# A two-part kernel (local attention and a state-space convolution): another element order in the tables that its K generator multiplies

## The chip, the cores and the metric

The kernel runs on one core of a Trainium2 chip. The metric is device time in microseconds: the median of three runs, and beside it one profiled execution with its trace. Engines are named as in the profile: PE is TensorE (matmuls), PEld its weight loads, DVE is VectorE, ACT is ScalarE, POOL is GpSimd and SP is SyncE, which issues most DMAs.

## What is computed

The reference has two independent halves, joined along the last axis. Half A is attention with 32 heads of 20 channels over a dilated window of 8 earlier positions (step 2). Half B is a convolution of the input with a kernel `K` that is itself a sum over 192 complex exponentials:

```python
logdA = dt * A                                  # 640 channels x 192 modes, complex
P = exp(logdA[:, :, None] * l[None, None, :])   # l = 0..2047
K = einsum("dn,dnl,dn->dl", Cc, P, dB).real     # 640 channels x 2048 positions
y = irfft(rfft(pad(u)) * rfft(pad(K)))[:L] + u * Dskip
```

The change touches only the computation of `K`.

## The kernel before

**Splitting of K.** A position l is written as a high and a low part (32 values times 64 values), so that exp(logdA·l) is a product of two tables. `Y` holds the 64 low positions and `X` the 32 high ones, each as a real and an imaginary part, for every mode and channel; the coefficients are folded into `X`. For one channel, `K` is then the matrix product of `X` and `Y` over the modes: 32 by 64 values.

**Chunks and steps.** The 640 channels are processed in five chunks of 128 (`c`), each as two halves of 64 (`th`). A half is 16 channels `t` in each of 4 groups `g`. The 192 modes of the four groups lie in 6 blocks of 128 partitions: blocks 0 to 3 hold modes 0 to 127 of one group each, blocks 4 and 5 hold the last 64 modes of two groups each. So per half the tables are `Y` [128, 2, 6, 64, 16] (real and imaginary, block, position, channel) and `X` [128, 2, 6, 16, 32] (channel outside, position inside).

**Table steps (`table_steps`, lines 185 to 267), 18 per half.** PE multiplies pieces of the parameters (`PM`, `PF`) with constant matrices (`RM`, `RF`, line 164 on) into PSUM (`ps_t`, two buffers), through `block` (lines 202 and 205). ACT turns that into tables:

- `gens` (line 215): exponentials `E`, two factors per block and channel.
- `mag(b)` (lines 222 to 226), three times, two blocks each: ACT writes magnitudes `M`, DVE multiplies them by `E` to get the other positions.
- `magx` (lines 235 and 236), two times (four blocks and two): magnitudes `MX` for X, the second half of the positions again by a DVE multiply with `E`.
- `sin(b, which, cs)` (line 248), twelve times: sines and cosines into `Y` or `X`. After the second of a pair DVE multiplies with the magnitudes: lines 254 to 256 for Y, line 260 for X.

**K steps (`kgen_steps`, lines 270 to 294), 8 per half.** For each channel t, part r and group g one matmul with 32 weight columns from `X` and 64 moving columns from `Y`, in one of four column groups of the array: line 286 for blocks 0 to 3, line 289 for blocks 4 and 5 with 64 rows. One half has 128 matmuls of each line. ACT copies the result to `Ksb` (line 292).

**What runs beside it.** `fwd_steps` (lines 376 and 387) and `inv_steps` (line 426) are the transforms of `u` and `K` as matmuls; `Evac` (line 337) copies PSUM to SBUF alternately on DVE and ACT; `prod` (line 417) multiplies spectra on DVE. Line 634 transposes the attention's input, line 654 is its projections, line 583 the last inverse step.

**Order.** `interleave` (line 342) mixes two lists of steps evenly in the program: the table steps of one half with the K steps of the half before and with transform steps (line 535). The framework's scheduler then fixes the order on each engine; `InOrder` (line 28) pins the order of ACT's table work, because ACT loads one function table for exponentials and another for sines. After some 362 us only attention and the last inverse step are left.

The address steps that matter here: at line 286 `rhs=Y[:, r, g, :, t]` walks the 64 positions with a step of 16 elements (32 bytes), and `lhsT=X[:, r, g, t]` takes 32 consecutive elements.

Of the kernel before, what the change touches and what calls it, by code (L numbers as in the profile page):

```python
# [10 lines left out]
A = mybir.AluOpType  # L11
ACT = mybir.ActivationFunctionType
AX = mybir.AxisListType
bf16 = mybir.dt.bfloat16
f32 = mybir.dt.float32
f16 = mybir.dt.float16
i16 = mybir.dt.int16
# [6 lines left out]
SINSC = 2.0 * 3.1415925 / 65536.0  # L24
ASC = 256.0
# [138 lines left out]
def table_consts_np():  # L164
    d = np.eye(16)
    j = np.arange(32)
    RF = np.zeros((128, 4, 512)); RM = np.zeros((128, 800))
    jt = lambda v: (v[None, :, None] * d[:, None, :]).reshape(16, -1)
    tj = lambda v: (v[None, None, :] * d[:, :, None]).reshape(16, -1)
    for cs in range(2):  # L170
        for r in range(2):
            RF[16 * r:16 * r + 16, cs] = jt(j + 0.5)
            sg = 1.0 if cs == 0 else -1.0
            RF[64 + 16 * r:80 + 16 * r, 2 + cs] = tj(sg * 64.0 * j)
            RF[96 + 16 * r:112 + 16 * r, 2 + cs] = tj(sg * np.ones(32))
        RF[32, cs] = RF[32, 2 + cs] = 3076.0 if cs == 0 else 3072.0
    l0 = np.concatenate([32 + np.arange(16), 15 - np.arange(16)])
    a = np.concatenate([jt(l0 / ASC), tj(64 * np.arange(16) / ASC), jt(np.array([16, 1024]) / ASC)], axis=1)
    for r in range(2):
        RM[16 * r:16 * r + 16] = a  # L180
        RM[32 + 16 * r:48 + 16 * r, 512:768] = tj(np.ones(16))
    return RF, RM


def table_steps(tc, pools, R, P, th, order, Y, X, rows=(128, 128), vorder=None):

    nc = tc.nc
    V = nc.vector  # L190
    MM = nc.tensor.matmul
    RF, RM = R
    PF, PM = P
    pool, psp = pools["arena"], pools["psum"]
    M = pool.tile([128, 6, 4, 256], bf16, name="M", tag="M", bufs=1)
    MX = pool.tile([128, 6, 16, 32], bf16, name="MX", tag="MX", bufs=1)
    E = pool.tile([128, 6, 2, 16], bf16, name="E", tag="E", bufs=1)
    steps = []

    def block(ps, blk, Pt, rhs, K=128):  # L200
        if blk < 4:
            MM(ps, lhsT=Pt[0:K, 2 * blk + th, 0:128], rhs=rhs[0:K], start=True, stop=True, skip_group_check=True)  # L202
        else:
            for h in range(2):
                MM(ps[64 * h:64 * h + 64], lhsT=Pt[0:K, 2 * (2 * h + blk - 4) + th, 128:192], rhs=rhs[0:K], start=True, stop=True,  # L205
                   tile_position=(0, 64 * h), skip_group_check=True)

    def new():
        return psp.tile([128, 2, 512], f32, name="ps_t", tag="tb", bufs=2)

    def gens():
        ps = new()
        for blk in range(6):
            block(ps[:, 0, 32 * blk:32 * blk + 32], blk, PM, RM[:, 768:800], rows[0])
        order(nc.scalar.activation(out=E[:].rearrange("p b k t -> p (b k t)"), in_=ps[:, 0, 0:192], func=ACT.Exp))

    def mag(b):
        def run():
            ps = new()
            for i in range(2):  # L220
                block(ps[:, i], 2 * b + i, PM, RM[:, 0:512], rows[0])
            order(nc.scalar.activation(out=M[:, 2 * b:2 * b + 2, 0:4:3], in_=ps[:].rearrange("p i (k x) -> p i k x", k=2), func=ACT.Exp))  # L222
            m4 = lambda k: M[:, 2 * b:2 * b + 2, k].rearrange("p b (j t) -> p b j t", t=16)
            e = E[:, 2 * b:2 * b + 2, 0].unsqueeze(2).to_broadcast([128, 2, 16, 16])
            V.tensor_tensor(out=m4(1), in0=m4(0), in1=e, op=A.mult)
            V.tensor_tensor(out=m4(2), in0=m4(3), in1=e, op=A.mult)
        return run

    def magx(b0, n):
        def run():  # L230
            ps = new()
            for i in range(n):
                block(ps[:, i // 2, 256 * (i % 2):256 * (i % 2) + 256], b0 + i, PM, RM[:, 512:768])
            lo = MX[:, b0:b0 + n, :, 0:16]
            order(nc.scalar.activation(out=lo, in_=ps[:].rearrange("p i (k t j) -> p (i k) t j", k=2, t=16)[:, 0:n], func=ACT.Exp))
            mxi = V.tensor_tensor(out=MX[:, b0:b0 + n, :, 16:32], in0=lo, in1=E[:, b0:b0 + n, 1].unsqueeze(3).to_broadcast([128, n, 16, 16]), op=A.mult)
            if vorder is not None:
                vorder(mxi)
        return run

    def sin(b, which, cs):
        def run():
            ps = new()
            for i in range(2):
                block(ps[:, i], 2 * b + i, PF, RF[:, 2 * which + cs], rows[1] if which == 0 else 128)
            bs = slice(2 * b, 2 * b + 2)
            dst = Y[:, cs, bs, 32:64].rearrange("p a j t -> p a (j t)") if which == 0 else X[:, cs, bs].rearrange("p a t j -> p a (t j)")
            order(nc.scalar.activation(out=dst, in_=ps[:].bitcast(i16)[:, :, 0::2], func=ACT.Sin, scale=SINSC))  # L248
            if cs == 1:
                if which == 0:  # L250
                    lo = Y[:, :, bs, 32:64].rearrange("p r a j t -> p r a (j t)")
                    hi = Y[:, :, bs, 0:32].rearrange("p r a j t -> p r a (j t)")
                    m = lambda k: M[:, bs, k:k + 2].rearrange("p a k x -> p a (k x)").unsqueeze(1).to_broadcast([128, 2, 2, 512])
                    V.tensor_tensor(out=hi, in0=lo, in1=m(0), op=A.mult)  # L254
                    V.tensor_scalar(out=lo[:, 1], in0=lo[:, 1], scalar1=-1.0, scalar2=None, op0=A.mult)
                    V.tensor_tensor(out=lo, in0=lo, in1=m(2), op=A.mult)  # L256
                else:
                    xf = X[:, :, bs].rearrange("p r a t j -> p r a (t j)")
                    mx = MX[:, bs].rearrange("p a t j -> p a (t j)").unsqueeze(1).to_broadcast([128, 2, 2, 512])
                    V.tensor_tensor(out=xf, in0=xf, in1=mx, op=A.mult)  # L260
        return run
    steps.append(gens)
    steps += [mag(b) for b in range(3)]
    steps += [magx(0, 4), magx(4, 2)]
    for b in range(3):
        steps += [sin(b, w, cs) for w in range(2) for cs in range(2)]
    return steps


def kgen_steps(tc, pools, th, Y, X, Ksb):  # L270
    nc = tc.nc
    MM = nc.tensor.matmul
    st = {}

    def part(jp, half, k0):
        def run():
            if half == 0 and k0 == 0:
                st[jp] = pools["psum"].tile([128, 8, 64], f32, name="ps_k", tag="k", bufs=2)
            ps = st[jp]
            for k in range(k0, k0 + 4):  # L280
                t = 8 * jp + k
                for r in range(2):
                    for g in range(4):
                        o = ps[32 * g:32 * g + 32, k, :]
                        if half == 0:
                            MM(o, lhsT=X[:, r, g, t], rhs=Y[:, r, g, :, t], start=(k == 0 and r == 0), stop=False, tile_position=(0, 32 * g), skip_group_check=True)  # L286
                        else:
                            hb = 64 * (g // 2)
                            MM(o, lhsT=X[hb:hb + 64, r, 4 + g % 2, t], rhs=Y[hb:hb + 64, r, 4 + g % 2, :, t], start=False, stop=(r == 1),  # L289
                               tile_position=(hb, 32 * g), skip_group_check=True)  # L290
            if half == 1 and k0 == 4:
                nc.scalar.copy(out=Ksb[:, 16 * th + 8 * jp:16 * th + 8 * jp + 8], in_=ps[:])
        return run
    return [part(jp, half, k0) for jp in range(2) for half in range(2) for k0 in (0, 4)]
# [139 lines left out]
def partB(tc, pools, prm, B_u, B_Dskip, out_b, att):  # L434
    nc = tc.nc
    MM = nc.tensor.matmul
    cn = fft_consts_np()
    usrc = B_u[0].rearrange("(l1 l0) (g ch) -> g l1 l0 ch", l0=64, g=4)
    with ExitStack() as outer:
# [5 lines left out]
        ar = pools["arena"]  # L445
        pools.update(psum=psk)
        order, vorder, sorder = InOrder(tc), InOrder(tc), InOrder(tc)
# [15 lines left out]
        RF, RM = R[:, 0:2048].rearrange("p (k x) -> p k x", k=4), R[:, 2048:2848]  # L463
# [19 lines left out]
        zedr()  # L483
        lnr()
        exp0()
        Y0 = lambda: ar.tile([128, 2, 6, 64, 16], bf16, name="Y0", tag="Y0")
        Y1 = lambda: ar.tile([128, 2, 6, 64, 16], bf16, name="Y1", tag="Y1")
        X0 = lambda: ar.tile([128, 2, 6, 16, 32], bf16, name="X0", tag="X0")
        X1 = lambda: ar.tile([128, 2, 6, 16, 32], bf16, name="X1", tag="X1")
        Yb, Xb = [Y0()], [X0()]  # L490
        fills = table_steps(tc, pools, (RF, RM), P, 0, order, Yb[0], Xb[0], rows=(32, 64), vorder=vorder)
        for st in fills[:6]:
# [394 lines left out]
```

## Time and profile before

| | us |
|---|---|
| median of three runs (573.23, 575.68, 578.89) | 575.68 |
| the profiled execution | 571.97 |
| its span | 570.2 |
| mean granted TensorE clock | 0.924 |

Busy time in the span: PE 430.1 us (75%) with 6929 matmuls, weight loads 266.7 (47%), DVE 410.3 (72%), ACT 342.3 (60%), POOL 35.2 (6%).

How to read it: no engine is full over the whole span, so a mean says little, and stages have to be looked at one by one. Rows of the groups name the line, engine and operation, output and inputs, size and count; behind the first bar come the total busy time and the mean duration of one, behind the second the idle time of the engine before them and what ended it. A PE row's duration is the latency of one matmul; matmuls overlap, so their pace is read from how many start in a stretch. The chain of waits of this trace reaches back to 260.5 us.

### The profile page before, as it was taken

The page shows a single profiled execution, that of the slowest core. Times are in us where ns is not written, and L with a number is a line of the kernel's source. Part 1 is how long each engine was busy: PE and PEld are TensorE (multiplying, and loading weights), DVE is VectorE, ACT ScalarE, POOL GpSimd, SP SyncE. Part 2 cuts the span into 40 slices and gives each one's busy share as a digit, 9 for nine tenths or more (in the row PEclk, how much of TensorE's full clock was granted, in tenths as well). Part 3 has the DMA queues.
Part 4 walks back from the last instruction along what each step waited for, and adds up shares of the span by engine and source line. Part 5 has one row for each costly group of instructions (what it writes and reads, how often), then busy time and mean ns, then how long its engine had stood idle before and what let it go on. Part 6 is the DMA issues. An engine that isn't in the chain of part 4 may idle for free.

```text
span 570.2 us, 15418 instructions
## 1 busy us (share of the span) xinstructions
PE 430.1 (75%) x6929; PEld 266.7 (47%) x6929; DVE 410.3 (72%) x501; ACT 342.3 (60%) x449; POOL 35.2 (6%) x49
## 2 busy tenths in 40 slices
PE   0135794798889798888988887899785679835796
PEld 0013463364556465546554555656552347701354
DVE  3574799869886998699976977232962669699880
ACT  2483683979597969595977595375221534421354
POOL 8700000000000000100000000000000000000000
PEclk9999997899899999899997999799798899955799
DMA  4594324350035203612052059205472150000112
GB/s 118 128 162 168 119 76 151 91 137 12 11 82 159 85 6 81 171 56 82 2 175 49 3 183 264 77 6 190 154 177 92 29 108 15 5 2 1 36 56 98
DMA packets 51674, 51.56 MB, mean 90 GB/s; under 512 B 37384, under 2 KB 48328, under 8 KB 48664
## 3 DMA queue, kind: packets, MB, share of 16 engines
q1 hardware_dynamic: 49720, 49.69, 31.9%
q0 software_dynamic: 1184, 0.89, 0.7%
q8 instruction: 54, 0.88, 0.6%
q10 hardware_dynamic: 704, 0.00, 0.1%
q14 instruction: 12, 0.10, 0.1%
HBM read 32.30 MB, written 18.19 MB: 89 GB/s over the span
## 4 chain that ended last, share of the span: by engine, by line
PE 29%; DVE 9%; ACT 7%; issue 6%; DMA 2%; SPq 0%; ACTq 0%; POOL 0%; DVEq 0%
PE ps_qk L654 7%; PE ps_v L693 4%; DVE prod L763 3%; PE ps_k L289 3%; PE ps_op L781 2%; DVE prod L706 2%; PE ps_k L286 2%; PE ps_ib L583 2%; ACT Y L248 2%; PE ps_l L709 2%; ACT X L248 1%; PE ps_ia L426 1%; PE ps_t L202 1%; PE ps_xt L634 1%; PE ps_ib L577 1%
## 5 line engine op out<-in xcount | busy, mean ns | idle before, releaser
L706 DVE TENSOR_TENSOR prod<-qT,kT 128x5120 bf16<-128x5120 bf16 x16 | 44.7, 2822 | 25.1 <-ACT kT L337 14.3
L248 ACT ACTIVATE X<-ps_t 128x1024 bf16<-128x1024 int16 x60 | 60.6, 1045 | 3.0 <-PE ps_t L202 2.3
L248 ACT ACTIVATE Y<-ps_t 128x1024 bf16<-128x1024 int16 x60 | 59.2, 1041 | 1.2 <-PE ps_t L202 0.6
L202 PE MATMUL ps_t<-R,PF 128*128 128x512 f16 (+1 forms) x160 | 51.8, 421 | 8.4 <-ACT X L248 3.7
L286 PE MATMUL ps_k<-Y,X 128*32 128x64 bf16 x1280 | 51.8, 294 | 2.1 <-issue 1.8
L289 PE MATMUL ps_k<-Y,X 64*32 64x64 bf16 x1280 | 47.7, 291 | 4.4 <-issue 2.4
L763 DVE TENSOR_TENSOR prod<-v,attn 128x2048 bf16<-128x2048 bf16 (+1 forms) x48 | 46.8, 1039 | 3.2 <-PE ps_o L767 2.7
L202 PE MATMUL ps_t<-R,PM 128*128 128x256 f16 (+4 forms) x120 | 23.4, 299 | 33.0 <-DMA PM<-scr 22.5
L337 DVE CAST A<-ps_f 128x1024 bf16<-128x1024 f32 x28 | 34.2, 1220 | 15.4 <-PE ps_f L376 15.2
L337 ACT CAST Ssp<-ps_f 128x1024 bf16<-128x1024 f32 x26 | 26.5, 1021 | 30.5 <-PE ps_f L387 23.1
L289 PEld LDWEIGHTS <-X 64*32 64x32 bf16 x1280 | 34.5, 109 | 19.3 <-issue 16.8
L286 PEld LDWEIGHTS <-X 128*32 128x32 bf16 x1280 | 34.2, 109 | 18.1 <-issue 11.6
L254 DVE TENSOR_TENSOR Y<-Y,M 128x2048 bf16<-128x2048 bf16 x30 | 36.6, 1219 | 6.1 <-ACT Y L248 6.0
L767 PE MATMUL ps_o<-prod,ident 32*32 32x512 bf16 (+1 forms) x768 | 22.5, 453 | 23.8 <-DVE prod L763 23.7
L376 PE MATMUL ps_f<-BD,u 128*64 128x128 bf16 x320 | 23.1, 296 | 22.9 <-DVE A L337 10.3
L256 DVE TENSOR_TENSOR Y<-Y,M 128x2048 bf16<-128x2048 bf16 x30 | 36.6, 1221 | 0.4
L260 DVE TENSOR_TENSOR X<-X,MX 128x2048 bf16<-128x2048 bf16 x30 | 36.6, 1219 | 0.2
L222 ACT ACTIVATE M<-ps_t 128x1024 bf16<-128x1024 f32 x30 | 30.0, 1026 | 8.8 <-DVE Y L256 4.3
L376 PEld LDWEIGHTS <-u 128*64 128x64 bf16 x320 | 20.8, 204 | 27.3 <-issue 27.1
L205 PE MATMUL ps_t<-R,PF 128*64 128x512 f16 (+1 forms) x160 | 25.4, 384 | 5.5 <-ACT Y L248 3.4
L202 PEld LDWEIGHTS <-PM 128*128 128x128 f16 (+1 forms) x120 | 8.6, 102 | 42.8 <-DMA PM<-scr 22.5
L337 DVE CAST Ssp<-ps_f 128x1024 bf16<-128x1024 f32 x14 | 17.1, 1220 | 12.6 <-PE ps_f L387 12.6
(150 smaller groups left out, 852.6 us busy)
## 6 DMA issues: line engine op xcount, KB each, us to landing
Udram<-Ssp SPq DMA_DIRECT2D x5, 1024.0 KB
U<-Udram SPq DMA_DIRECT2D x5, 1024.0 KB
Uw<-Udram SPq DMA_DIRECT2D x10, 512.0 KB
Zdram<-Z SPq DMA_DIRECT2D x5, 1024.0 KB
zq<-Zdram SPq DMA_DIRECT2D x25, 192.0 KB
u<-in_B_u_dram SPq DMA_DIRECT2D x4, 640.0 KB
xn<-in_A_x_dram SPq DMA_DIRECT2D x4, 640.0 KB
out_dram<-ob SPq DMA_DIRECT2D x16, 160.0 KB
```

What stands on the lines that cost most here:

```text
L202: MM(ps, lhsT=Pt[0:K, 2 * blk + th, 0:128], rhs=rhs[0:K], start=True, stop=True, skip_group_check=True)
L248: order(nc.scalar.activation(out=dst, in_=ps[:].bitcast(i16)[:, :, 0::2], func=ACT.Sin, scale=SINSC))
L254: V.tensor_tensor(out=hi, in0=lo, in1=m(0), op=A.mult)
L256: V.tensor_tensor(out=lo, in0=lo, in1=m(2), op=A.mult)
L260: V.tensor_tensor(out=xf, in0=xf, in1=mx, op=A.mult)
L286: MM(o, lhsT=X[:, r, g, t], rhs=Y[:, r, g, :, t], start=(k == 0 and r == 0), stop=False, tile_position=(0, 32 * g), skip_group_check=True)
L289: MM(o, lhsT=X[hb:hb + 64, r, 4 + g % 2, t], rhs=Y[hb:hb + 64, r, 4 + g % 2, :, t], start=False, stop=(r == 1), tile_position=(hb, 32 * g) ...
L337: ins = self.nc.scalar.copy(out=out, in_=in_) if e == "a" else self.nc.vector.tensor_copy(out=out, in_=in_)
L376: MM(ps[64 * r:64 * r + 64, i], lhsT=src_fn(8 * q + i), rhs=BD[:, r], start=(i % 4 == 0), stop=True, skip_group_check=True, tile_position= ...
L654: self.nc.tensor.matmul(ps, lhsT=self.w[w][:, kt, 128 * ct:128 * ct + 128], rhs=rhs(kt), start=(kt == 0), stop=(kt == 4))
L706: self.nc.vector.tensor_tensor(out=pr[:], in0=q4[:, :, :, hs], in1=k4[:, :, :, hs], op=A.mult)
L763: nc.vector.tensor_tensor(out=p2[:, 0:nd], in0=self.v2[:, 8 * b:8 * b + nd, off:off + 256], in1=self.attn[:, hf, w, :].unsqueeze(1).to_bro ...
```

## The change

All tables get a common order: quads of channels outermost (24 quads: 6 blocks of 4), then positions, then the 4 channels of a quad innermost. The constant matrices are permuted to match (`tjt`), and the E table is ordered by factor, then quad, then channel. At the K step the channel becomes `4 * g + t // 4` and `t % 4`.

```diff
-    M = pool.tile([128, 6, 4, 256], bf16, name="M", tag="M", bufs=1)
-    MX = pool.tile([128, 6, 16, 32], bf16, name="MX", tag="MX", bufs=1)
-    E = pool.tile([128, 6, 2, 16], bf16, name="E", tag="E", bufs=1)
+    M = pool.tile([128, 2 * (6 * 512 + 64)], bf16, name="M", tag="M", bufs=1)
+    MX = pool.tile([128, 24, 32, 4], bf16, name="MX", tag="MX", bufs=1)
+    E = pool.tile([128, 2, 24, 4], bf16, name="E", tag="E", bufs=1)
...
     def mag(b):
...
-            for i in range(2):
-                block(ps[:, i], 2 * b + i, PM, RM[:, 0:512], rows[0])
...
-            m4 = lambda k: M[:, 2 * b:2 * b + 2, k].rearrange("p b (j t) -> p b j t", t=16)
-            e = E[:, 2 * b:2 * b + 2, 0].unsqueeze(2).to_broadcast([128, 2, 16, 16])
-            V.tensor_tensor(out=m4(1), in0=m4(0), in1=e, op=A.mult)
-            V.tensor_tensor(out=m4(2), in0=m4(3), in1=e, op=A.mult)
+            for q in range(2):
+                for i in range(2):
+                    block(ps[:, q, 256 * i:256 * i + 256], 2 * b + i, PM, RM[:, 256 * q:256 * q + 256], rows[0])
...
+            e = E[:, 0, 8 * b:8 * b + 8].unsqueeze(2).to_broadcast([128, 8, 16, 4])
+            for o, i in ((64, 0), (3072, 3136)):
+                m = lambda x: M[:, 1024 * b + x:1024 * b + x + 1024].rearrange("p (k j t) -> p k j t", j=32, t=4)[:, :, 0:16]
+                V.tensor_tensor(out=m(o), in0=m(i), in1=e, op=A.mult)
...
     def magx(b0, n):
...
-            mxi = V.tensor_tensor(out=MX[:, b0:b0 + n, :, 16:32], in0=lo, in1=E[:, b0:b0 + n, 1].unsqueeze(3).to_broadcast([128, n, 16, 16]), op=A.mult)
+            mxi = V.tensor_tensor(out=MX[:, 4 * b0:4 * b0 + 4 * n, 16:32], in0=lo, in1=E[:, 1, 4 * b0:4 * b0 + 4 * n].unsqueeze(2).to_broadcast([128, 4 * n, 16, 4]), op=A.mult)
...
     def sin(b, which, cs):
...
-                    lo = Y[:, :, bs, 32:64].rearrange("p r a j t -> p r a (j t)")
-                    hi = Y[:, :, bs, 0:32].rearrange("p r a j t -> p r a (j t)")
-                    m = lambda k: M[:, bs, k:k + 2].rearrange("p a k x -> p a (k x)").unsqueeze(1).to_broadcast([128, 2, 2, 512])
+                    lo = Y[:, :, ks, 32:64].rearrange("p r k j t -> p r k (j t)")
+                    hi = Y[:, :, ks, 0:32].rearrange("p r k j t -> p r k (j t)")
+                    m = lambda q: M[:, 3072 * q + 1024 * b:3072 * q + 1024 * b + 1024].rearrange("p (k z) -> p k z", z=128).unsqueeze(1).to_broadcast([128, 2, 8, 128])
...
-                            MM(o, lhsT=X[:, r, g, t], rhs=Y[:, r, g, :, t], ...)
+                            MM(o, lhsT=X[:, r, 4 * g + t // 4, :, t % 4], rhs=Y[:, r, 4 * g + t // 4, :, t % 4], ...)
...
-        Y0 = lambda: ar.tile([128, 2, 6, 64, 16], bf16, name="Y0", tag="Y0")
+        Y0 = lambda: ar.tile([128, 2, 24, 64, 4], bf16, name="Y0", tag="Y0")
...
-        X0 = lambda: ar.tile([128, 2, 6, 16, 32], bf16, name="X0", tag="X0")
+        X0 = lambda: ar.tile([128, 2, 24, 32, 4], bf16, name="X0", tag="X0")
```

So at the K step both operands are now read with a step of 4 elements (8 bytes): Y's 64 positions (32 bytes before) and X's 32 positions (consecutive before). A magnitude step issues twice as many matmuls of half the width (256 columns). `Y1` and `X1` change like `Y0` and `X0`, the second K matmul like the first, and `sin`'s output and the multiplication of X follow the new shapes. The numbers of DVE and ACT instructions stay the same.

## The prediction

> **What bounds the kernel now.** I read the costliest groups first, then the timeline of PE for the pace of single matmul runs, then the busy time of all engines between the loads of ScalarE's function table, then the chain of waits. The first fence has the page's span line and its two rows of the K generator, then three rows of the list of groups with shapes kept apart.
>
> ```profile
> span 570.2 us, 15418 instructions
> ...
> L286 PE MATMUL ps_k<-Y,X 128*32 128x64 bf16 x1280 | 51.8, 294 | 2.1 <-issue 1.8
> ...
> L289 PE MATMUL ps_k<-Y,X 64*32 64x64 bf16 x1280 | 47.7, 291 | 4.4 <-issue 2.4 <-DVE Y L256 2.0
> ...
> L225 DVE TENSOR_TENSOR M<-M,E 128x512 bf16<-128x512 bf16 x30 | 12.6, 420 | 10.7 <-ACT M L222 10.6
> ...
> L236 DVE TENSOR_TENSOR MX<-MX,E 128x1024 bf16<-128x1024 bf16 x10 | 12.2, 1220 | 3.0 <-ACT MX L235 3.0
> L236 DVE TENSOR_TENSOR MX<-MX,E 128x512 bf16<-128x512 bf16 x10 | 6.8, 684 | 1.4 <-ACT MX L235 1.4
> ```
>
> 2560 matmuls of only 64 columns. A row's mean is a latency, and four column groups run at once, so the pace has to come from the timeline: start, length, engine, line, count.
>
> ```profile
> 202.87 1.57 PE L286 MATMUL ps_k<-Y,X 128*32 128x64 bf16 x45
> ...
> 224.35 1.11 PE L376 MATMUL ps_f<-BD,u 128*64 128x128 bf16 x16
> ...
> 371.38 0.64 PE L376 MATMUL ps_f<-BD,Ksb 128*64 128x128 bf16 x16
> ...
> 457.14 2.39 PE L583 MATMUL ps_ib<-zq,H 32*32 32x160 bf16 x128
> ```
>
> Taking off the last matmul's latency gives the pace. K: (1.57 - 0.30)/44 = 28.9 ns, or 115 ns for a group of four tiles. Line 583, also four tiles with 32 weight columns each: (2.39 - 0.24)/127 = 16.9 ns, 68 ns per four, although it streams 160 columns against K's 64. Line 583 reads consecutive columns; K reads Y with a step of 32 bytes. Line 376 shows the same on the weights: 64 columns taken from u with a step of 320 bytes go at (1.11 - 0.30)/15 = 54 ns, from Ksb, where they are consecutive, at (0.64 - 0.23)/15 = 27 ns. So widely stepped reads slow PE here: 115 ns for 64 columns is 1.8 ns a column.
>
> Where this matters the windows tell. ScalarE alternates between the exponential table (E, M, MX) and the sine table. Columns: length, then busy us of PE, PE weight load, DVE, ACT, POOL, and the granted clock.
>
> ```profile
> 73.85:99.71 25.86, 18.44 (x362) 13.47 (x359) 24.27 (x64) 14.46 (x22) 1.38 (x1) 0.84 0.31 96
> 114.86:126.25 11.39, 11.39 (x255) 7.89 (x255) 7.26 (x11) 8.07 (x10) 0.52 (x1) 1.00 0.52 146
> 126.25:138.96 12.71, 9.39 (x104) 4.35 (x103) 10.67 (x11) 12.63 (x14) 0.00 (x0) 1.00 0.23 35
> 138.96:155.96 17.00, 14.94 (x306) 10.18 (x306) 15.16 (x23) 10.20 (x12) 1.25 (x1) 0.90 0.02 4
> 172.44:183.75 11.31, 11.31 (x238) 8.07 (x230) 7.61 (x12) 8.49 (x11) 0.00 (x0) 1.00 0.59 149
> 198.93:213.56 14.63, 13.69 (x294) 9.68 (x287) 13.60 (x22) 10.11 (x13) 1.25 (x1) 1.00 0.02 5
> 229.81:243.41 13.60, 11.06 (x212) 7.76 (x200) 9.10 (x8) 7.58 (x10) 0.00 (x0) 0.87 0.55 131
> 258.84:274.60 15.76, 14.73 (x311) 9.95 (x314) 13.95 (x19) 9.49 (x12) 0.00 (x0) 1.00 0.11 35
> 274.60:288.54 13.94, 12.05 (x146) 7.21 (x142) 13.82 (x17) 13.90 (x16) 0.00 (x0) 1.00 0.01 1
> 288.54:300.83 12.29, 10.48 (x234) 7.08 (x230) 6.75 (x11) 7.59 (x10) 0.00 (x0) 0.95 0.78 231
> 316.34:333.41 17.07, 15.01 (x306) 10.19 (x306) 15.19 (x23) 10.20 (x13) 0.00 (x0) 0.90 0.01 2
> 346.20:362.60 16.40, 13.99 (x315) 10.49 (x315) 7.69 (x8) 6.14 (x8) 0.04 (x1) 0.90 0.82 245
> ```
>
> The two sine stretches shown (from 126.25 and 274.60) have ACT busy 99%; the other sine stretches 86 to 98%. Few K matmuls lie there (4 to 72 in each by the counts of lines 286 and 289). The other ten rows are the exponential stretches and the last one, and they hold almost all of K: by the same counts 252, 218, 252, 174, 240, 158, 229, 202, 252 and 252 matmuls. In them ACT has room, and PE or DVE is the full engine. In the last, the chain of waits is half K:
>
> ```profile
> by line: PE ps_k L289 26.7%; PE ps_k L286 24.3%; PE ps_xt L634 18.7%; issue 13.9%; ACT Y L248 10.5%; PE ps_t L205 4.6%; PE ps_f L376 3.9%; PE ps_qk L654 1.8%
> ```
>
> **The change, part by part.**
>
> Y is read with 8 bytes instead of 32. No row has PE reading at 8 bytes, so I bound it. Not better: 115 ns per four, if the slow pace belongs to any step. Best: 64/160 of line 583's 68 ns, 27 ns. Between: if two neighbouring columns together cost what one costs now, 115/2 = 58 ns. Weights bound it too: line 376 with Ksb loads two times 64 columns in 55 ns, so four times 32 columns need about 55 as well if they go one after another. I take 60 ns, 15.0 ns per matmul, near line 583's 16.9, the only four-tile row without a step. That saves 13.9 ns each, 35.6 us of PE over 2560.
>
> [...]
>
> X's weights go from consecutive to a step of 8 bytes. At best free. At worst each column pays like u's: 54 ns for 64 columns is 27 ns for 32, still under today's 28.9 per matmul. So this edit can take the gain away, but cannot by itself make K slower. I take it as covered by the streaming.
>
> MX's multiply (line 236) now has four consecutive E values innermost instead of one repeated. 1024 elements cost 1220 ns now; the product with U at line 417, the same size but consecutive, costs 688, and 512 elements at line 225 cost 420 against 684. If four-element rows count as consecutive, a table set saves 0.53 + 0.26 = 0.80 us of DVE. Lines 225 and 226 have the opposite risk: their E rows shrink from 16 elements to four. Bounds: nothing, or 684 instead of 420, 0.26 us x 60 = 16 us of DVE. I take nothing, since the 16-element rows already run at the fast price.
>
> The Y multiplies go from rows of 512 to rows of 128, same elements. The casts of A (rows of 8) and Ssp (rows of 256) both cost 1220 ns, so row length is free. ScalarE's outputs change pattern, not size: M in pieces of 256 costs 1026 ns, X in one piece 1045; zero.
>
> Magnitude matmuls: 80 of 512 columns become 160 of 256. From zero (same columns) to 80 x 27 ns = 2.2 us; I take 1 us.
>
> The built program has the same instructions otherwise, in an order that shifts in places, on SP only around the writes of Ssp and the pieces. Like stretches differ today by about 1.2 us around their mean (11.3 to 13.6; 14.6 to 17.1); nine of them with random signs make 3.6, so 4 us either way.
>
> Sum. Each stretch can gain at most the K saving, DVE's idle time plus the 0.8 of MX, or ACT's idle time, whichever is least. From 73.85: 2.4 (DVE), 3.0, 2.6 (DVE), 2.4, 1.8 (DVE), 2.2, 2.6 (DVE), 2.8, 2.7 (DVE), 3.5; together 26.0 us. An engine driven to zero idle is not what in-order queues give, so I take in full only the three where PE holds the end (114.86, 172.44 and the last: 8.9), and half of the five under DVE (12.1) and of the two where PE itself idles 15 to 19% (5.0): 8.9 + 6.0 + 2.5 = 17.4. Less 1 for the split: 16.4. The sine stretches gain nothing; after 362.6 us no part of the change is left. The profiled execution took 571.97 us (span 570.2 plus 1.8 around it), 3.7 below the median of 575.68. So 555.6 against it, 559 on the median's scale. What is late next is DVE's multiply of Y (line 256), for which K's second half waits already (2.0 us in its row).
>
> **The rivals.**
>
> Nothing on PE: X's stepped weights, or the 8-byte step itself, keep 115 ns. Then only MX is left, 0.8 us in five stretches under DVE, half of it, 2 us: 574. For it: a weight load one after another at u's rate costs as much as now. Against: u's step is 320 bytes.
>
> More: reading at 27 ns and weights in parallel. K saves 22 ns each; limits then give 3.3 + 2.8 + 5.6 in the PE stretches and 10 in the others: 21.7, so about 555, and 546 if all caps of 26 and the spread of 4 come together.
>
> Slower: the clock. If shorter K bursts leave PE idle and its clock is cut, every consecutive stream is slower. PE's busy time from 74 to 362.6 us is 245.5, of it 82 K, so 164 scale with the clock, whose mean there is 0.94. At 0.70 that is 164 x (0.94/0.70 - 1) = 56 us, half on the path 28, less 16.4: 587. It decides from a mean of 0.78 down (34 us, half 17). For it: 0.52 and 0.62 are seen between 500 and 540 us, where PE starves. Against: the row with PE's lowest share among those shown for sines, 126.25 at 74%, has clock 1.00.
>
> [...]
>
> **How the numbers follow.** Forecast 0.62 (551 to 567), more 0.12, nothing 0.16, slower 0.10. From the 26 us ceiling plus spread, 546, rounded to 547, up to 577 (574 and the spread of the runs shown, about 3): only the slower case and the tails lie outside. About 1%, 5.8 us, is what a measurement can tell: faster 0.74, same 0.16, slower 0.10.
>
> **What would show it.** K runs at 14 to 17 ns per matmul, and exponential stretches 1 to 3 us shorter while sine stretches stay; the 1024-element MX multiply near 690 ns, M's near 420; X's weight loads not much above 109 ns; clock near 0.94 until 362 us. It is wrong if K stays at 28 ns, or if K is fast and the stretches keep their length because DVE's line 256 ends them, or if M's multiplies cost 680.

## The result, and the profile after

The changed kernel takes 556.01 us (median of 4 runs, 555.12 to 558.34), the kernel before, run beside it, 574.45 us (4 runs): a ratio of 0.9715 with an interval of 0.9636 to 0.9794. A second comparison on another chip, with more runs, gave 0.9778 [0.9730, 0.9826], 557.41 against 569.79 us. Ratios compare means and leave out every run more than 1.5% above the fastest of its kernel, so they are not the quotients of the medians. The profiled execution took 555.12 us; the kernel before had 571.97 in its own.

First the page of the changed kernel: its span and the two K rows (busy us, mean ns of one, then the idle time before them).

```profile
span 553.3 us, 15581 instructions
...
L288 PE MATMUL ps_k<-Y,X 128*32 128x64 bf16 x1280 | 31.7, 240 | 4.4 <-issue 2.4
...
L292 PE MATMUL ps_k<-Y,X 64*32 64x64 bf16 x1280 | 27.6, 234 | 4.3 <-issue 2.8
```

K had 51.8 + 47.7 = 99.5 us of PE before and has 59.3 now. The list of groups with shapes kept apart has the multiplies of DVE and X's weight loads:

```profile
L228 DVE TENSOR_TENSOR M<-M,E 128x512 bf16<-128x512 bf16 x60 | 22.3, 418 | 4.2 <-ACT M L224 3.8
...
L238 DVE TENSOR_TENSOR MX<-MX,E 128x1024 bf16<-128x1024 bf16 x10 | 6.9, 688 | 2.9 <-ACT MX L237 2.9
L238 DVE TENSOR_TENSOR MX<-MX,E 128x512 bf16<-128x512 bf16 x10 | 4.2, 416 | 1.0 <-ACT MX L237 1.0
...
L288 PEld LDWEIGHTS <-X 128*32 128x32 bf16 x1280 | 22.8, 118 | 16.8 <-issue 9.3 <-DVE X L262 3.7 <-DVE Y L258 0.8
```

MX's multiplies fell from 1220 and 684 ns to 688 and 416, M's stayed at 418. The timeline of PE has the pace (start, length, engine, line, count, and the idle time before, if any):

```profile
308.99 1.42 PE L288 MATMUL ps_k<-Y,X 128*32 128x64 bf16 x79
...
311.98 1.15 PE L292 MATMUL ps_k<-Y,X 64*32 64x64 bf16 x64 [0.52 <-DVE Y L258]
```

(1.42 - 0.24)/78 = 15.1 ns per matmul for the first half of K, (1.15 - 0.23)/63 = 14.6 for the second, against 28.9 before. The second line also shows what K waits for now: DVE's second multiply of Y.

The busy time of all engines in the nine exponential stretches, and last from the start of the first of them to the last K matmuls, with all that lies between (length, PE, PE weight load, DVE, ACT, POOL, granted clock, DMA share, GB/s):

```profile
74.83:102.09 27.26, 18.05 (x396) 13.79 (x393) 24.85 (x65) 14.98 (x22) 1.41 (x1) 0.81 0.31 91
117.13:125.32 8.19, 6.29 (x218) 4.65 (x218) 5.04 (x10) 6.47 (x8) 0.56 (x1) 1.00 0.96 233
138.35:152.96 14.61, 11.15 (x316) 8.71 (x316) 14.34 (x23) 9.78 (x12) 1.38 (x1) 1.00 0.03 7
168.91:180.89 11.98, 11.65 (x304) 8.86 (x303) 8.19 (x13) 9.21 (x12) 0.16 (x1) 1.00 0.55 146
193.86:208.36 14.50, 11.20 (x316) 8.79 (x316) 14.21 (x23) 9.78 (x12) 1.38 (x1) 1.00 0.03 7
224.30:233.70 9.40, 8.38 (x225) 6.44 (x225) 8.53 (x5) 7.31 (x10) 0.17 (x1) 0.82 0.79 202
249.92:262.18 12.26, 10.02 (x258) 7.22 (x258) 12.26 (x19) 9.32 (x12) 0.00 (x0) 1.00 0.01 3
276.08:284.28 8.20, 7.24 (x221) 5.21 (x219) 6.04 (x11) 7.27 (x9) 0.00 (x0) 1.00 0.83 288
301.73:317.65 15.92, 12.55 (x321) 10.07 (x321) 13.96 (x22) 9.78 (x12) 0.00 (x0) 0.79 0.01 3
...
74.83:347.00 272.17, 211.15 (x4172) 143.76 (x4168) 228.31 (x313) 216.49 (x247) 12.38 (x9) 0.94 0.35 99
```

Set against the rows of before, stretch by stretch, in us:

| stretch | 1 | 2 | 3 | 4 | 5 | 6 | 7 | 8 | 9 | sum |
|---|---|---|---|---|---|---|---|---|---|---|
| before | 25.86 | 11.39 | 17.00 | 11.31 | 14.63 | 13.60 | 15.76 | 12.29 | 17.07 | 138.9 |
| after | 27.26 | 8.19 | 14.61 | 11.98 | 14.50 | 9.40 | 12.26 | 8.20 | 15.92 | 122.3 |
| change | +1.40 | -3.20 | -2.39 | +0.67 | -0.13 | -4.20 | -3.50 | -4.09 | -1.15 | -16.6 |

All of the gain is in the exponential stretches. The sine stretches between and before them together went from 155.2 to 156.1 us. From the last load of the sine table to the end of the last K matmul it took 28.9 us before and 29.6 after, and from there to the end of the span 208 and 206. So K's tail, in which half of the chain of waits was K, is no shorter. Stretch 5 is as long as it was: DVE is busy 14.21 of its 14.50 us, and PE, busy 11.20 us there for 13.69 before, spends idle what the faster K saves it.

### The profile page after: what moved, and what is told of

Read it like the earlier page. It is cut to its first block, busy times and chain, and to the rows that moved or that the text cites. A ratio compares the mean times of both kernels' runs of the same rounds, so it can differ in the third digit from the quotient of the medians.

```text
span 553.3 us, 15581 instructions
## 1 busy us (share of the span) xinstructions
PE 397.3 (72%) x7009; PEld 254.0 (46%) x7009; DVE 401.4 (73%) x501; ACT 339.5 (61%) x449; POOL 35.2 (6%) x49
## 5 line engine op out<-in xcount | busy, mean ns | idle before, releaser
L709 DVE TENSOR_TENSOR prod<-qT,kT 128x5120 bf16<-128x5120 bf16 x16 | 44.7, 2822 | 27.4 <-ACT kT L340 14.5
L250 ACT ACTIVATE Y<-ps_t 128x1024 bf16<-128x1024 int16 x60 | 59.3, 1042 | 1.7 <-PE ps_t L203 0.9
L340 DVE CAST A<-ps_f 128x1024 bf16<-128x1024 f32 x28 | 34.1, 1218 | 22.5 <-PE ps_f L379 22.5
L203 PE MATMUL ps_t<-R,PM 128*128 128x256 f16 (+3 forms) x160 | 23.3, 265 | 35.8 <-DMA PM<-scr 23.5
L256 DVE TENSOR_TENSOR Y<-Y,M 128x2048 bf16<-128x2048 bf16 x30 | 36.5, 1217 | 7.4 <-ACT Y L250 7.4
L258 DVE TENSOR_TENSOR Y<-Y,M 128x2048 bf16<-128x2048 bf16 x30 | 36.6, 1219 | 0.3
L288 PE MATMUL ps_k<-Y,X 128*32 128x64 bf16 x1280 | 31.7, 240 | 4.4 <-issue 2.4
L203 PEld LDWEIGHTS <-PM 128*128 128x128 f16 (+1 forms) x160 | 13.2, 100 | 43.0 <-DMA PM<-scr 23.5
L292 PE MATMUL ps_k<-Y,X 64*32 64x64 bf16 x1280 | 27.6, 234 | 4.3 <-issue 2.8
L288 PEld LDWEIGHTS <-X 128*32 128x32 bf16 x1280 | 22.8, 118 | 16.8 <-issue 9.3
L429 PE MATMUL ps_ia<-IA,U 128*128 128x128 bf16 x160 | 23.4, 227 | 4.7 <-DVE Z L340 3.5
L203 PEld LDWEIGHTS <-PF 128*128 128x128 f16 (+1 forms) x160 | 14.0, 102 | 27.8 <-issue 22.1
```

The source lines that it names most:

```text
L258: V.tensor_tensor(out=lo, in0=lo, in1=m(1), op=A.mult)
L288: MM(o, lhsT=X[:, r, 4 * g + t // 4, :, t % 4], rhs=Y[:, r, 4 * g + t // 4, :, t % 4], start=(k == 0 and r == 0), stop=False, tile_positio ...
L292: MM(o, lhsT=X[hb:hb + 64, r, kq, :, t % 4], rhs=Y[hb:hb + 64, r, kq, :, t % 4], start=False, stop=(r == 1), tile_position=(hb, 32 * g), s ...
L340: ins = self.nc.scalar.copy(out=out, in_=in_) if e == "a" else self.nc.vector.tensor_copy(out=out, in_=in_)
L709: self.nc.vector.tensor_tensor(out=pr[:], in0=q4[:, :, :, hs], in1=k4[:, :, :, hs], op=A.mult)
```

## The experiments

Three questions stand behind the gain of 13 to 16 us (by the two ratios). Is it K's pace, and what in the read sets that pace? Is it MX's multiply? Is it the order of the instructions? The last one can't be left aside: a different operand step also makes the build put the instructions in a different order. Two orders matter below. "The changed order" is that of the changed kernel. "The other order" is the one that came about where X's weights were read consecutively, or at 32 bytes, with Y at 8 or 32; some 1330 of the 7009 matmul places differ between the two (here and below: the matmuls in order of time, told apart by the names of what they write and read).

Most variants change only what K's matmuls read, by one helper that cuts a channel's 64 (or 32) positions out of the same table with a step of n elements; n = 4 is the changed kernel's own read:

```python
def steps_y(Y, ps, r, b, t, n):
    f = lambda a, w: Y[ps, r, a:a + w].rearrange("p k j t -> p (k j t)")
    if n == 16:
        return f(4 * b, 4)[:, t::16]
    if n == 8:
        return f(4 * b + 2 * (t // 8), 2)[:, t % 8::8]
    q = f(4 * b + t // 4, 1)
    if n == 4:
        return q[:, t % 4::4]
    m = q.shape[1] // 4 * n
    o = m * ((t % 4) // n)
    return q[:, o + t % n:o + m:n]
```

Each diff below shows the first half of K; the second half has the same edit.

**Y at 32 bytes, X at 8, in the changed order.**

```diff
-rhs=Y[:, r, 4 * g + t // 4, :, t % 4]
+rhs=steps_y(Y, slice(0, 128), r, g, t, 16)
```

> The changed kernel, but K's moving operand is taken from Y with a step of 32 bytes again (the elements read are others, so K's values are not the reference's; counts, sizes and the order on every engine are those of the changed kernel). Theory, the pace of K is the gain: K returns to 27 to 29 ns per matmul and the time to about 572 us (574.5 before, less 2 for MX), ratio 0.99 to 1.00. Rival, the cheaper MX multiply on DVE or the new order on the engines is the gain: K is slow again but the time stays within 555 to 562 us, ratio below 0.98.

Measured: 569.33 us (10 runs) against 569.24, ratio 1.0009 [0.9972, 1.0046]. The timeline of PE in this kernel shows K back at the old pace, (2.59 - 0.30)/78 = 29.4 ns:

```profile
320.93 2.59 PE L302 MATMUL ps_k<-Y,X 128*32 128x64 bf16 x79
```

All the other parts of the change are in this kernel: MX's cheap multiply (687 ns), the split magnitude matmuls, the new order. Together they are worth nothing that these runs resolve (2 us either way). What the change gains hangs on the step of Y.

**Y at 16 bytes**, a single run:

```diff
-rhs=steps_y(Y, slice(0, 128), r, g, t, 16)
+rhs=steps_y(Y, slice(0, 128), r, g, t, 8)
```

> The changed kernel with Y read with a step of 16 bytes (other elements, so K's values are not the reference's; same counts and order). Theory, neighbouring columns share a fetch of 16 bytes: 16 bytes is as slow as 32, 27 to 29 ns per matmul. Rival, the cost grows with the step: between 15 and 28, about 19 ns. Second rival, weights set the changed kernel's pace and the reading is free up to some step: 14 to 16 ns.

Measured: 567.67 us. Half the step, the same pace, (2.57 - 0.30)/78 = 29.1 ns:

```profile
321.75 2.57 PE L302 MATMUL ps_k<-Y,X 128*32 128x64 bf16 x79
```

**Y and X consecutive:**

```diff
-MM(o, lhsT=X[:, r, 4 * g + t // 4, :, t % 4], rhs=Y[:, r, 4 * g + t // 4, :, t % 4],
+MM(o, lhsT=steps_y(X, slice(0, 128), r, g, t, 1), rhs=steps_y(Y, slice(0, 128), r, g, t, 1),
```

> The changed kernel with both K operands read consecutively (other elements, so K's values are not the reference's; same counts, the scheduler shifts the order a little). Theory, reading Y two columns to a fetch sets the 14 to 15 ns: K falls below 14, to 7 if streaming alone were left. Rival, four weight loads one after another set it (13.8 ns each by the Ksb row): K stays at 13 to 15 ns. On the time: if PE still holds the stretches, another 3 us per ns 1.2 saved, 550 to 553 us at 10 ns; if DVE and ACT have taken over, 555 to 557.

Measured: 547.11 us (4 runs), ratio 0.9611 [0.9570, 0.9652], with K at (0.73 - 0.20)/68 = 7.8 ns, in an order that differs from the other one in some 950 places.

```profile
327.24 0.73 PE L302 MATMUL ps_k<-Y,X 128*32 128x64 bf16 x69
```

This is 6 to 10 us below the changed kernel by the ratios, but two things changed with it, the pace and the order. The next runs part them.

**Y consecutive, X left at 8 bytes**, a single run:

```diff
-rhs=Y[:, r, 4 * g + t // 4, :, t % 4]
+rhs=steps_y(Y, slice(0, 128), r, g, t, 1)
```

> The changed kernel with Y read consecutively and X still with a step of 8 bytes (Y's elements are others, so K's values are not the reference's; same counts, order shifted a little). With both consecutive K went at 7.8 to 9.2 ns. Theory, the four weight loads run side by side and are hidden: again 8 to 10 ns. Rival, X's step costs as much as Y's did: 13 to 15 ns as in the changed kernel.

Measured: 562.26 us against 570.33. K is as fast as with both consecutive, (0.69 - 0.205)/59 = 8.2 ns, and yet the kernel is slower than the changed one. The timeline of PE, and the windows over the table stretches (columns as above):

```profile
316.93 0.69 PE L302 MATMUL ps_k<-Y,X 128*32 128x64 bf16 x60
```

```profile
74.50:355.30 280.80, 211.60 (x4168) 139.84 (x4166) 228.84 (x313) 217.97 (x247) 12.35 (x9) 0.87 0.33 96
```

X's weights with a step of 8 bytes don't hold K at 15 ns. The granted clock is 0.87 here where the changed kernel has 0.94. Some 270 of the matmul places differ from the changed order, so this single run doesn't tell the clock from the order.

**Channel pairs instead of quads, in the changed order to the instruction.** All tables have pairs innermost, so that both operands are read with a step of 4 bytes.

```diff
-    tjt = lambda v: (v[None, None, :, None] * d.reshape(16, 4, 1, 4)).reshape(16, -1)
+    tjt = lambda v: (v[None, None, :, None] * d.reshape(16, 8, 1, 2)).reshape(16, -1)
...
-    MX = pool.tile([128, 24, 32, 4], bf16, name="MX", tag="MX", bufs=1)
-    E = pool.tile([128, 2, 24, 4], bf16, name="E", tag="E", bufs=1)
+    MX = pool.tile([128, 48, 32, 2], bf16, name="MX", tag="MX", bufs=1)
+    E = pool.tile([128, 2, 48, 2], bf16, name="E", tag="E", bufs=1)
...
-MM(o, lhsT=X[:, r, 4 * g + t // 4, :, t % 4], rhs=Y[:, r, 4 * g + t // 4, :, t % 4],
+MM(o, lhsT=X[:, r, 8 * g + t // 2, :, t % 2], rhs=Y[:, r, 8 * g + t // 2, :, t % 2],
```

> The same change with channel pairs in place of quads: 48 pairs outermost, then positions, then 2 channels, so K reads both operands with a step of 4 bytes. Nothing is left out. Theory, cost by fetches of 16 bytes, now four columns each: 8 to 10 ns per matmul, as fast as consecutive, and the multiplies by E, with rows of two, keep 418 and 688 ns: 547 to 551 us, faster than the changed kernel by about 1%. Rival, rows of two elements lose the packed rate on DVE (684 and 1220 ns, 24 us more): 556 us or more. On the time a second rival, PE no longer matters: 555 to 557.

Measured: 560.69 us (6 runs), ratio 0.9818 [0.9774, 0.9863], no better than the quads (0.9778 on another chip), and above both the 547 to 551 us of the theory and the 555 to 557 of the second rival. K runs at (0.83 - 0.20)/78 = 8.1 ns; M's and MX's multiplies keep their price (419, 689 and 420 ns). The timeline, then the windows of one exponential stretch (the fifth) and of all:

```profile
311.39 0.83 PE L288 MATMUL ps_k<-Y,X 128*32 128x64 bf16 x79
```

```profile
194.10:208.70 14.60, 10.38 (x315) 7.51 (x315) 14.08 (x22) 9.99 (x12) 1.04 (x1) 0.88 0.02 4
...
74.40:350.00 275.60, 202.98 (x4171) 134.54 (x4170) 229.20 (x313) 217.41 (x247) 12.35 (x9) 0.90 0.34 98
```

PE is 8 us less busy than after the change (203.0 against 211.2), and the stretches together are 3.4 us longer. The fifth has DVE full in both kernels (14.08 of 14.60, 14.21 of 14.50), so a faster K has little to give there. And the clock is lower: 0.90 over all, 0.88 in the fifth, where it was 1.00. How much of the missing gain is DVE and how much the clock was not told apart.

**Single channels outermost**, both operands consecutive, and every row of E one repeated element (the same edit as for pairs, with one channel):

```diff
-    tjt = lambda v: (v[None, None, :, None] * d.reshape(16, 4, 1, 4)).reshape(16, -1)
+    tjt = lambda v: (v[None, None, :, None] * d.reshape(16, 16, 1, 1)).reshape(16, -1)
```

> The same change with single channels outermost, so K reads both operands consecutively and E's innermost row is one repeated element. Nothing is left out. K goes at 8 to 9 ns as with consecutive reads. Theory, the multiplies by E lose the packed rate: 684 ns for M, 1220 and 684 for MX, 24 us of DVE in the exponential stretches, of which a third to two thirds shows: 555 to 565 us, slower than pairs. Rival, DVE has room: 547 to 551 us, like pairs.

Measured: 562.18 us (6 runs), ratio 0.9823 [0.9772, 0.9874]. The list of groups shows M's multiplies at the price that the prediction had as their upper bound:

```profile
L228 DVE TENSOR_TENSOR M<-M,E 128x512 bf16<-128x512 bf16 x60 | 38.0, 685 | 5.4 <-ACT M L224 5.3
```

They cost 15.7 us more of DVE than after the change, MX's (1218 and 684 ns) 8 more. The time lies in the expected range, but it is not slower than pairs, as had been expected. Against the kernel with the same consecutive reads and cheap multiplies (0.9611), the ratio is 0.021 higher, 12 us. That would make DVE worth about half its price, but the orders of these two were not matched, and below an order alone is worth 5 to 9 us; so what DVE's 24 us cost in time is not shown. Shown is that rows of four or of two E values are what keeps M cheap (418 and 419 ns, for 685 here).

**MX's multiply dear again**, all else as changed:

```diff
-in1=E[:, 1, 4 * b0:4 * b0 + 4 * n].unsqueeze(2).to_broadcast([128, 4 * n, 16, 4])
+in1=E[:, 1, 4 * b0:4 * b0 + 4 * n, 0:1].unsqueeze(2).to_broadcast([128, 4 * n, 16, 4])
```

> The changed kernel with MX's multiply reading one repeated E element innermost, as before the change (the factor of each first channel of a quad for all four, so MX is not the reference's). It should cost 1220 and 684 ns again, 8 us more of DVE. Theory, MX is a small part of the gain: 557 to 560 us. Rival, the stretches are bound by DVE now (it is busy 98% of two of them): 5 us or more, 561 us and up.

Measured: 557.41 us (4 runs), ratio 0.9807 [0.9744, 0.9871], with MX at the old price:

```profile
L238 DVE TENSOR_TENSOR MX<-MX,E 128x1024 bf16<-128x1024 bf16 x10 | 12.2, 1221 | 2.9 <-ACT MX L237 2.9
```

Of the changed kernel's two ratios, 0.9778 lies inside that interval and 0.9715 just below it, with an interval of its own up to 0.9794. MX's multiply is worth less than these runs resolve, and some 280 matmul places moved with it.

**The changed kernel again**, beside the next three on one chip:

> The changed kernel itself once more, to stand beside the next three on one chip and beside pairs. Theory, K's pace is worth 16 to 17 us in this order: ratio to before 0.97. If pairs (0.982) are really slower than quads, it lies below 0.977; if that was chance, near 0.98.

Measured: 557.41 us (6 runs) against 569.79 (17 runs), ratio 0.9778 [0.9730, 0.9826]. That is between the two values expected; whether pairs are really slower than quads stays open.

**X consecutive, Y at 8 bytes, in the other order:**

```diff
-MM(o, lhsT=X[:, r, 4 * g + t // 4, :, t % 4],
+MM(o, lhsT=steps_y(X, slice(0, 128), r, g, t, 1),
```

> The changed kernel with X's weights read consecutively (other elements, so K's values are not the reference's). In the built program every engine has the same work, but in the order of the run with X at 32 bytes, which is nearer to that of the kernel before. Theory, the step of X's weights costs nothing on PE but turned the scheduler to a worse order: K at 14 to 15 ns as in the changed kernel and yet 547 to 551 us. Rival, the one look at 550 us was chance: 555 to 557 us, as the changed kernel.

Measured: 548.97 us (6 runs), ratio 0.9614 [0.9559, 0.9668]. K's pace in its timeline is (1.26 - 0.24)/68 = 15.0 ns:

```profile
325.33 1.26 PE L302 MATMUL ps_k<-Y,X 128*32 128x64 bf16 x69
```

The same pace as the changed kernel, 8.4 us less; and the same ratio as with both consecutive (0.9611), where K ran at 7.8 ns, so below 15 ns nothing more came out here either, though these two orders differ in some 950 places. X's 8-byte step costs PE nothing that can be seen, but its edit changed the order, and the order costs.

**X consecutive, Y at 32 bytes, in the other order to the instruction:**

```diff
-rhs=Y[:, r, 4 * g + t // 4, :, t % 4]
+rhs=steps_y(Y, slice(0, 128), r, g, t, 16)
```

(and X as in the run before)

> As the last, with X consecutive and Y at 32 bytes (other elements, so K's values are not the reference's): the order of the last run to the instruction, K at its old pace of 27 to 29 ns. Theory, pace and order add: 563 to 567 us, 4 to 6 below the kernel with the changed order and the old pace, and 15 to 17 above the last run. Rival, the order is only better with a fast K: 568 to 571, as the kernel before.

Measured: 564.75 us (10 runs), ratio 0.9914 [0.9879, 0.9949], K at (2.29 - 0.29)/68 = 29.4 ns:

```profile
341.63 2.29 PE L302 MATMUL ps_k<-Y,X 128*32 128x64 bf16 x69
```

With this run the two causes stand in a square (ratios to the kernel before, 29 ns on the left, 15 on the right; the upper row has X at 8 bytes, the lower X consecutive):

| | Y at 32 bytes | Y at 8 bytes | pace |
|---|---|---|---|
| changed order | 1.0009 | 0.9778 | 13 us |
| other order | 0.9914 | 0.9614 | 17 us |
| order | 5 us | 9 us | |

The intervals of the four ratios leave 3 to 4 us either way on each difference. So pace and order are both clear of the noise, and whether the order is worth more with a fast K is not.

**X at 32 bytes, Y at 8**, a single run, in the other order:

```diff
-MM(o, lhsT=X[:, r, 4 * g + t // 4, :, t % 4],
+MM(o, lhsT=steps_y(X, slice(0, 128), r, g, t, 16),
```

> The changed kernel with X's weights read with a step of 32 bytes and Y with 8 (X's elements are others, so K's values are not the reference's; same counts and order). Theory, weights and Y are read side by side, and 32 lone fetches of 1.8 ns take 58 ns, as long as Y's 64 columns in pairs: 14 to 17 ns per matmul. Rival, weight loads of the four column groups share one reader: 4 x 58 ns per four, 50 ns or more per matmul; or they add to Y's reading: 25 to 30 ns.

Measured: 550.26 us against 570.33. The list of groups and the timeline of PE:

```profile
L302 PEld LDWEIGHTS <-X 128*32 128x32 bf16 x1280 | 28.7, 163 | 13.4 <-issue 6.8 <-DVE X L262 2.9 <-DVE Y L258 0.8
```

```profile
329.10 1.39 PE L302 MATMUL ps_k<-Y,X 128*32 128x64 bf16 x69
```

A weight load takes 163 ns where the consecutive one (X consecutive, Y at 8 bytes) has 108, and K goes at (1.39 - 0.245)/68 = 16.8 instead of 15.0 ns. The changed kernel, with X at 8 bytes, has 118 and 15.1 ns: four times the step on the weights costs 2 ns, and the same on Y 14. The time goes with the order and not with X's step: with the dearest weight loads of all it is 0.965 of the kernel before, like X consecutive (0.961) and unlike X at 8 bytes in the changed order (0.978). So the order, and not the step of X, parts the two rows of the square, as far as a single run can tell.

**Y, M and E in quads, X and MX in single channels.** It keeps Y's 8-byte step, gives X its consecutive read back, and pays for it with MX's dear multiply.

```diff
+    tjx = lambda v: (v[None, None, :, None] * d.reshape(16, 16, 1, 1)).reshape(16, -1)
...
-    MX = pool.tile([128, 24, 32, 4], bf16, name="MX", tag="MX", bufs=1)
+    MX = pool.tile([128, 96, 32, 1], bf16, name="MX", tag="MX", bufs=1)
...
-MM(o, lhsT=X[:, r, 4 * g + t // 4, :, t % 4],
+MM(o, lhsT=X[:, r, 16 * g + t // 1, :, t % 1],
...
-        X0 = lambda: ar.tile([128, 2, 24, 32, 4], bf16, name="X0", tag="X0")
+        X0 = lambda: ar.tile([128, 2, 96, 32, 1], bf16, name="X0", tag="X0")
```

> Y, M and E as in the changed kernel, but X and MX with single channels outermost and positions innermost, so X's weights are consecutive again and nothing is left out. MX's multiply costs 1220 and 684 ns again, 8 us more of DVE. The order is within 191 of 7009 matmul places that of the two runs before. Theory, order is worth more than MX's multiply: 549 to 554 us, faster than the changed kernel. Rival, MX's multiply takes back what the order gives: 555 to 558 us.

Measured: 549.84 us (6 runs), ratio 0.9658 [0.9608, 0.9708]: 7.6 us below the changed kernel on the same chip, and below both kernels, though MX costs 1222 and 685 ns again. K runs at (1.14 - 0.24)/62 = 14.5 ns, and the stretches show the old clock:

```profile
328.26 1.14 PE L290 MATMUL ps_k<-Y,X 128*32 128x64 bf16 x63
```

```profile
73.00:340.00 267.00, 210.75 (x4180) 139.43 (x4177) 236.34 (x314) 218.80 (x249) 12.51 (x10) 0.94 0.36 102
```

DVE does 8 us more than after the change (236.3 against 228.3), and from the first exponential stretch to the last K matmul it takes 264.8 us instead of 272.4: the better order gives more than MX's multiply takes.

## Why the prediction was right, and where it was not

**K's pace.** The step that carried the forecast was the choice of 60 ns per four tiles, because "two neighbouring columns together cost what one costs now". The trace after has 15.1 and 14.6 ns for 15.0. The runs show the same thing as a law of this case: 29 ns at 32 and at 16 bytes, 15 at 8, and 8 both at 4 bytes and consecutive. That fits a cost by the number of 16-byte pieces that the columns lie in, 29 ns for 64 of them, half for 32, and a floor near 8 ns for 16 and for 8; it is a reading of these steps alone. Where a piece begins and what makes the floor were not tried.

**The other reason for the 60 was wrong.** "Weights bound it too", at about 55 ns per four, does not hold: in pairs K takes 4 x 8.1 = 32 ns per four, and with Y consecutive and X still at 8 bytes 4 x 8.2 = 33. That bound agreed with the right value by chance.

**X's weights, taken as covered.** They are: K's pace is the same with X consecutive (15.0 ns). But X's edit was not free. It came with another order, and between the two orders lie 5 to 9 us, more than any term of the sum but K's.

**MX, M, Y, ScalarE, the split magnitude matmuls.** 688, 416 and 418 ns for the forecast 688, 420 and 420; the Y multiplies 1217 and 1219; ACT's X in 1047. With K slow again all of this together, order included, gave 1.0009, so the 2 us that were left for MX alone and the 1 us against the split are inside the noise or cancelled by the order.

**The order, 4 us either way.** For the order that was built this held: with a slow K, order and all other parts together are worth nothing (1.0009). As a measure of what an order can do it was too small. It was taken from how much like stretches differ, with random signs; between the two orders it is 5 us with a slow K and 9 with a fast one, and the sign is one that the build decides.

**The caps.** The sum, 16.4 us, and 555.6 us against the profiled execution, met 555.12. Its parts did not meet theirs. That an engine keeps some idle time, from which the halves were taken, was an estimate: DVE is busy 12.26 of 12.26 us in stretch 7 after the change. The first two rows set the prediction's terms, stretch by stretch, against the kernel before and the one after. That difference mixes pace with order. The last two hold the order fixed: from Y at 32 bytes to the changed kernel, and in the other order from Y at 32 to Y at 8 with X consecutive. All are us gained, read from the loads of the function tables; the changed kernel's repeat differs by up to 1.0 us in a stretch.

| stretch | 1 | 2 | 3 | 4 | 5 | 6 | 7 | 8 | 9 | sum | sine stretches between | tail |
|---|---|---|---|---|---|---|---|---|---|---|---|---|
| predicted | 1.2 | 3.0 | 1.3 | 2.4 | 0.9 | 1.1 | 1.3 | 1.4 | 1.4 | 14.0 | 0 | 3.5 |
| before to after | -1.4 | 3.2 | 2.4 | -0.7 | 0.1 | 4.2 | 3.5 | 4.1 | 1.1 | 16.6 | 0.2 | -0.6 |
| pace, changed order | 2.7 | 0.2 | 0.9 | 2.5 | 0.8 | 1.4 | 1.0 | 1.4 | -0.2 | 10.7 | 3.2 | 0.4 |
| pace, other order | 1.8 | 2.4 | 1.6 | 0.3 | 0.9 | 0.9 | 1.4 | 1.4 | 2.1 | 12.8 | 2.4 | 0.5 |

With the order held, the pace gave 11 to 13 us in the exponential stretches for the 14 counted, 2 to 3 us in the sine stretches, for which nothing was counted, and half a microsecond in the tail for 3.5. That the total was met is in part luck: the sine stretches made up for most of the tail. The gains of 4.2, 3.5 and 4.1 us in stretches 6, 7 and 8, above their caps of 2.2, 2.6 and 2.8, are mostly the order: with a slow K in the changed order these stretches already take 10.85, 13.29 and 9.55 us, where they had 13.60, 15.76 and 12.29, because work moved between stretches (DVE has 5 instructions in the sixth, where it had 8). The fourth, taken in full because PE was full in it, did gain 2.5 from the pace in the changed order; the new order hid it.

**The tail.** The step that failed is its 3.5 us "in full". The chain of waits named K as half of it, and K at half its time left the length nearly as it was: from the last load of the sine table to the last K matmul 30.0 us with Y at 32 bytes in the changed order (30.2 at 16) and 29.6 after (28.9 in the repeat), 26.4 and 25.9 in the other order; the kernel before, in an order of its own, took 28.9. The order has a share in the length, 3 to 4 us: the other kernels in the changed order or near it take 28.6 to 28.9, all others after the change 25.0 to 26.7. What took K's saving can be read in the two traces of the changed order. From the first K matmul after the wait for X (348.48 and 335.14 us) to the end of the last one both take 12.1 us. With the slow K, PE is busy 11.7 of them, with the fast one 8.1, and at one and the same matmul of the transposes it stands still for 0.4 us in the first and 3.5 us in the second:

```profile
356.95 0.23 PE L651 MATMUL ps_xt<-ident,xn 128*128 128x128 bf16 x1 [0.40 <-issue]
...
344.34 0.25 PE L637 MATMUL ps_xt<-ident,xn 128*128 128x128 bf16 x1 [3.52 <-issue]
```

In the other order it is 0.6 us with the slow K and 3.0 with the fast one, again at one place in the order:

```profile
350.00 0.75 PE L306 MATMUL ps_k<-Y,X 64*32 64x64 bf16 x18 [0.63 <-issue]
...
334.04 0.46 PE L306 MATMUL ps_k<-Y,X 64*32 64x64 bf16 x18 [3.00 <-issue]
```

So K gave PE the time back (some 250 matmuls at 14 ns, 3.6 us), and PE stood still for most of it. The 13.9% "issue" in the prediction's chain of waits is for the most part such a standstill, of 2.1 us ahead of 356.42 us; the sum took no account of it. What it may be stands in the last section.

**What is late next** was named rightly in part. DVE is full in stretches 3, 5 and 7 (14.34 of 14.61, 14.21 of 14.50, 12.26 of 12.26 us), and the pairs show that K below 15 ns has nothing more to give in this order. But the wait that was named, for DVE's second multiply of Y (line 256 before, 258 now), is 1.6 us in the row of K's second half, less than its 2.0 before, and "issue" in that row has 2.8.

**The rivals.** "Nothing on PE" is refuted by the pace, and the run with Y at 32 bytes shows what it would have been: no change, 1.0009, where 574 of 575.68 (0.997) had been worked out. "More" came about in the pairs as far as the reading goes, 32 ns per four, but its further gain of 4 us did not. "Slower by the clock" did not happen, 0.94 before and after, but a lower clock comes with a shorter K: 0.90 in pairs, 0.87 with Y consecutive, 0.91 with both consecutive. A low clock comes without a single long gap too: in the kernel before, PE is busy 1.38 of the 3.41 us from 145.89 on, idle in pieces of at most 1.5 us, and the granted clock of the next 3.41 us is 0.50. PE's busy time alone does not settle it: from 466.75 on it is 1.38 of 3.41 us as well, and the clock stays at 1.00. What the lower clock costs in time was not told apart; with both consecutive the kernel is one of the two fastest all the same.

## What to carry to other kernels

Lay out a matmul's moving operand so that the columns of one read lie close together: here 1, 2 and 4 columns to 16 bytes gave 29, 15 and 8 ns, while on the weights, with X consecutive at 15.0 ns, a step of 8 bytes gave 15.1 and one of 32 bytes 16.8. Take such a layout change apart by operand: keep the step on the one that needs it, and leave the other as it was. Before a layout is judged by its time, look at whether the build put the instructions in another order with it; here that was worth 5 to 9 us, a third to a half of what the layout itself gave. And a saving on one engine counts only where that engine does not then wait for something else: in the tail PE had K's 3.6 us back and stood still for most of them.

## What was not expected of the hardware

**Sixteen bytes.** That 32 and 16 bytes cost the same to within 0.3 ns, and 8 half, was not in any row of the kernel before.

**A gap and the clock after it.** In the tail PE stands still for 3.5 us in the middle of eight matmuls of line 637, waiting for nothing that the profile shows ("issue"), while the DMAs move 282 GB/s. The windows around it, in the changed kernel:

```profile
338.00:340.80 2.80, 2.32 (x87) 1.78 (x75) 1.22 (x1) 1.11 (x2) 0.00 (x0) 1.00 1.00 239
340.80:344.30 3.50, 0.03 (x1) 0.00 (x0) 0.00 (x0) 0.00 (x0) 0.00 (x0) 1.00 0.83 282
344.30:346.00 1.70, 1.63 (x37) 1.39 (x37) 0.00 (x0) 0.58 (x1) 0.00 (x0) 0.54 0.13 39
346.00:348.00 2.00, 2.00 (x66) 1.40 (x65) 1.23 (x1) 0.58 (x1) 0.16 (x1) 0.54 0.00 0
348.00:350.00 2.00, 2.00 (x21) 1.07 (x19) 0.17 (x1) 1.50 (x2) 0.00 (x0) 1.00 0.00 0
```

After it the granted clock is 0.54 for 3.7 us (0.50 from 344.42 to 347.84 us) and then 1.00 again. The repeat has a gap of 3.0 us in the same place, and its granted clock is 0.79, 0.50 and 0.86 in the three stretches of 2 us from 344 us on; pairs have a gap of 1.9 us there. In the kernel before, the standstill of 2.1 us that ends at 356.42 us is followed by 0.50 from 357.52 to 360.93 us. Whether the gap itself lowers the clock was not tried.

What PE stands still for was not tried. The traces have a candidate: transfers of 16384 bytes and kind "instruction" on DMA queue 8, 54 before and 55 after, one for some 255 matmuls and weight loads. One of them runs from 341.75 to 342.88 us, inside the gap of the changed kernel. Between 60 and 500 us the profile puts six gaps of PE over 1.4 us down to "issue", three before and three after. For every one of them such a transfer starts at most 1.0 us before the gap or 0.9 us into it; with one transfer in some 9 us, chance would give that to about a fifth of them. In the three runs after the change with Y at 32 or 16 bytes PE has no such gap from 290 to 400 us, the longest is 1.1 us. That PE waits there for its own instructions, which a faster K uses up sooner while the DMA engines are busy with other loads, fits all of this, but it is argued and not shown.
